# Two products instead of three for mixture-of-experts tiles of at most 64 rows, chosen by branches on TensorE, VectorE and ScalarE

## The chip, the cores and the metric

One core of one Trainium2 chip runs the whole program. The metric is the device time of one execution in microseconds, median of three runs. The traces come from one further, profiled execution.

## The reference, cut to what matters

An attention block with a memory term gives 2304 rows of 512 numbers. Two mixture-of-experts layers follow; each sends every row to one of 8 experts and scales the expert's result by a gate:

```python
expert_idx = np.argmax(logits, axis=1)
gate_w = probs[np.arange(N), expert_idx]
for e in range(E):
    mask = expert_idx == e
    h = np.maximum(x[mask] @ w1[e], 0.0)      # 512 -> 1024
    out[mask] = gate_w[mask, None] * (h @ w2[e])   # 1024 -> 512
```

On the inputs used, the reference sends these numbers of rows to the experts: layer 1: 14, 70, 440, 370, 0, 749, 11, 650; layer 2: 104, 380, 548, 438, 276, 112, 310, 136.

## The kernel before, in words

The attention part comes first. Then each layer (L = 0 and 1) runs in steps of one tile: 128 rows of one expert, gathered by index. The experts' rows are padded to whole tiles, so each layer has 22 tiles on these inputs. The largest expert comes first, the second largest last, the others in order of their index. The program is written for up to 28 steps a layer; from step 18 on each step stands in a branch on the real number of tiles (lines 1646 and 1726).

Products are made in three parts to keep float32's accuracy: each operand is split into a high part and a low rest, and the product is high x Wh, high x Wl, low x Wh. `mms` (line 1253) issues them: 4 blocks of the inner dimension times 3 for each half of the hidden layer (24 matmuls of 128x128 by 128x512 into `ph0` and `ph1`), and 8 blocks times 3 (24 matmuls into `py`). The plane of the weights (two are kept) is chosen at run time by a register, `pv`, so each matmul has a register operation ahead of it (lines 1219 and 1253).

A step of `step()` in order, on TensorE: 12 matmuls into `ph0`; 6 into `ph1`; four transposes of the first hidden half (`hT(0)`, line 1365); in layer 1 four transposes of the last result for the second layer's routing (`yT_pe`, line 1306); 6 more into `ph1`; four transposes of the next tile's rows (`xT_pe`, line 1192); 3 matmuls into `py`; `hT(1)`; 21 matmuls into `py`. ScalarE applies ReLU from PSUM (lines 1395 and 1416) and writes high parts (line 1196), VectorE writes low parts (line 1197), both also split the next expert's weights (lines 903 and 906). `end()` scales `py` into `ysb` on ScalarE (line 1355) and GpSimd sends it out: to a scratch tensor in layer 1, by an indirect DMA to the result in layer 2.

The order of the work on each engine is the order of the program text (a manual schedule); the framework places the semaphores. The weights' splits and loads stand in branches on flags held in registers (lines 1264, 1280, 1284). The registers are loaded from bit words in `fw` (line 1202) at steps 4 and 16. In the trace `PEldq`, `ACTq` and `DVEq` are the sequencers, the parts of the engines that run register operations, branches and semaphore instructions; their time isn't counted as busy.

Of the kernel before, what the change touches and what calls it, by code (L numbers as in the profile page):

```python
# [389 lines left out]
def tile_kernel(ctx, tc, q, k, v, M_prev, z_prev, beta, emb, tau, w1a, w2a, wg, w1b, w2b, out):  # L390
# [4 lines left out]
    P = 128  # L395
# [43 lines left out]
    fw = ctile([P, 2, 3], "fw", I32)  # L439
# [287 lines left out]
    def finish1(L, NI, psc, psi, new, st):  # L727
# [3 lines left out]
        ci = rtile([P, E], "ci", I32)  # L731
# [17 lines left out]
        V.tensor_copy(nt, ci)  # L749
        yield  # L750
# [75 lines left out]
    def finish2(L, st):  # L826
# [7 lines left out]
        V = nc.vector  # L834
        stt, ts = V.scalar_tensor_tensor, V.tensor_scalar
# [8 lines left out]
        V.tensor_tensor(out=c8, in0=c8, in1=ea.unsqueeze(1).to_broadcast([P, E, E]), op=ALU.mult)  # L844
        V.tensor_tensor(out=w["mo"], in0=s0, in1=nt, op=ALU.add)
        V.tensor_reduce(out=w["code"], in_=c8, axis=AX.X, op=ALU.add)
# [333 lines left out]
    class Bufs:  # L1180


        def __init__(self, where):
            self.x = (where(0), where(1))
            self.h = ((where(2), where(3)), (where(4), where(5)))
            self.hs = (where(6), where(7))
# [7 lines left out]
    def hilo(ps, hl):  # L1194
        hi, lo = hl
        nc.scalar.activation(out=hi, in_=ps, func=AF.Copy)  # L1196
        nc.vector.tensor_tensor(out=lo, in0=ps, in1=hi.bitcast(F32), op=ALU.subtract)  # L1197

    NK = (KD, KF)

# [5 lines left out]
    class Step:  # L1206


        def __init__(self, L, t):
            self.L, self.t = L, t  # L1210
            if 0 < t <= NE:
                self.pv = steps[L, 0].pv
            elif t:
                g, k = divmod(t - TW, BW)
                if k == 0:
                    self.words = words(fw[0:1, g, 0:3], [ACT_, DVE_, POOL_]) + words(fw[0:1, g, 2:3], [PE_])
                else:
                    self.words = steps[L, t - 1].words
                self.pv = nc.snap((self.words[3] >> k) & 1, engines=[PE_], min_val=0, max_val=1)
            else:  # L1220
                self.pv = 0 if L == 0 else nc.values_load(ini[0:1, 1, 4:5], engines=[PE_], min_val=0, max_val=1)
            self.spl = [[], []]

# [20 lines left out]
        def mms(self, i, ps, lhs, n0, qs, first=False, last=False):  # L1244
            L, t = self.L, self.t
            ps_ = slice(self.pv, self.pv + 1) if isinstance(self.pv, int) else bass.ds(self.pv, 1)
            for q_ in qs:
                kk, m = divmod(q_, 3)
                hi, lo, col = lhs(kk)
                w = 1024 * kk + n0 if i == 0 else 512 * kk  # L1250
                W = (Wh, Wl, Wh)[m][i][:, ps_, w:w + 512].rearrange("p o n -> p (o n)")
                x = (hi, hi, lo)[m]
                mm = nc.tensor.matmul(ps, x[:, col:col + P], W, start=(first and q_ == qs[0]), stop=(last and q_ == qs[-1]))  # L1253
# [6 lines left out]
            self.lm = (i, mm.ins)  # L1260

        def splits(self, i, cs, parts="hl"):

            with tc.If(self.fv[i] > 0):  # L1264
                for c in cs:
                    for x in parts:
# [5 lines left out]
                        if last_mm.get(i) is not None:  # L1272
                            tc.add_manual_dep(ins, last_mm[i].name, SYNC, reason="buffer free")
# [89 lines left out]
    def hT(i, b):  # L1363
        for kk in range(4):
            nc.tensor.transpose(pts[i][:, P * kk:P * kk + P], b.hs[i][:, P * kk:P * kk + P], ident)  # L1365
        hilo(pts[i], b.h[i])
# [5 lines left out]
    def next_step(L, t):  # L1372
        n = steps[L, t] = Step(L, t)
# [3 lines left out]
    def step(L, t):  # L1377
# [7 lines left out]
        lx = lambda kk: (*x, P * kk)  # L1385
        lh = lambda kk: (*b.h[kk // 4], P * (kk % 4))
        begin(L, t)
        s.gemm(0, ph0, lx, 0, 0, 3)
        yield
        s.gemm(0, ph0, lx, 0, 3, 9)  # L1390
        yield
        s.gemm(0, ph0, lx, 0, 9, 12)
        if split2:
            s.splits(0, (0, 1))
        nc.scalar.activation(out=b.hs[0], in_=ph0, func=AF.Relu)
# [8 lines left out]
        s.gemm(0, ph1, lx, 512, 0, 6)  # L1404
        hT(0, b)
# [8 lines left out]
        s.gemm(0, ph1, lx, 512, 6, 12)  # L1414
        last_mm[0] = s.lm[1]
        nc.scalar.activation(out=b.hs[1], in_=ph1, func=AF.Relu)
# [6 lines left out]
        if more:  # L1423
            hilo(psx, b.x)
        if rt2:
            route2_iov()
        s.gemm(1, py, lh, 0, 0, 3)
        if split2:
            s.splits(0, (2,), "h")
        hT(1, b)  # L1430
        if split2:
            s.splits(0, (2,), "l")
        if more:
            next_step(L, t + 1)
        yield
        s.gemm(1, py, lh, 0, 3, 6)
# [8 lines left out]
        s.gemm(1, py, lh, 0, 6, 9)  # L1445
# [23 lines left out]
        for q_ in range(9, 24, 3):  # L1469
            yield  # L1470
            s.gemm(1, py, lh, 0, q_, q_ + 3)
        last_mm[1] = s.lm[1]
# [24 lines left out]
    def flags_words(st):  # L1497
        yield
        x = rtile([P, 2, 3], "fx3", BF16)
        nc.vector.tensor_tensor(out=x, in0=st["fl"][:, 4:7].unsqueeze(1).to_broadcast([P, 2, 3]), in1=pw.unsqueeze(2).to_broadcast([P, 2, 3]), op=ALU.mult)  # L1500
        yield
        nc.tensor.matmul(pm1[:, 400:406], ones, x.rearrange("p g i -> p (g i)"), start=True, stop=True)
        nc.vector.tensor_copy(fw.rearrange("p g i -> p (g i)"), pm1[:, 400:406])
# [56 lines left out]
    b = Bufs(lambda i: Wh[0][:, 1, 512 * i:512 * i + 512] if i < 6 else None)  # L1560
    s = steps[0, 0] = Step(0, 0)
    lx = lambda kk: (*b.x, P * kk)
    lh = lambda kk: (*b.h[kk // 4], P * (kk % 4))
# [29 lines left out]
    x0 = tuple(fp.tile([P, 512], F32R, name=f"x0{i}") for i in range(2))  # L1593
# [3 lines left out]
    bufs = Bufs(lambda i: fp.tile([P, 512], F32R, name=f"b{i}") if i < 6 else hs_[i - 6])  # L1597
# [4 lines left out]
    nc.scalar.activation(out=b.hs[0], in_=ph0, func=AF.Relu)  # L1602
    nc.scalar.activation(out=b.hs[1], in_=ph1, func=AF.Relu)
# [25 lines left out]
    last_mm[0] = last_mm[1] = s.lm[1]  # L1629
# [21 lines left out]
    lx = lambda kk: (*x0, P * kk)  # L1651
    lh = lambda kk: (*b.h[kk // 4], P * (kk % 4))
# [45 lines left out]
    nc.scalar.activation(out=b.hs[0], in_=ph0, func=AF.Relu)  # L1698
# [59 lines left out]
```

## Time and profile before

| | |
|---|---|
| median of 3 runs | 886.68 us (885.24 to 887.39) |
| the profiled execution's own time | 885.27 us |
| its span, first to last instruction | 883.5 us |
| TensorE busy | 854.2 us, 97% of the span |
| TensorE's mean granted clock | 0.993 |
| VectorE, ScalarE, GpSimd busy | 508.7, 473.8, 276.9 us |

The profiled execution's time is 1.8 us above its span and 1.4 us below the median. TensorE's busy share is taken over pipelined matmuls whose ends are modelled, so what a step costs is better read from the distance between the starts of two steps.

### The profile page before, as it was taken

The page shows a single profiled execution, that of the slowest core. Times are in us where ns is not written, and L with a number is a line of the kernel's source. Part 1 is how long each engine was busy: PE and PEld are TensorE (multiplying, and loading weights), DVE is VectorE, ACT ScalarE, POOL GpSimd, SP SyncE. Part 2 cuts the span into 40 slices and gives each one's busy share as a digit, 9 for nine tenths or more (in the row PEclk, how much of TensorE's full clock was granted, in tenths as well). Part 3 has the DMA queues.
Part 4 walks back from the last instruction along what each step waited for, and adds up shares of the span by engine and source line. Part 5 has one row for each costly group of instructions (what it writes and reads, how often), then busy time and mean ns, then how long its engine had stood idle before and what let it go on. Part 6 is the DMA issues. An engine that isn't in the chain of part 4 may idle for free. (4 is left out here: it accounts for less than half of the span.)

```text
span 883.5 us, 20598 instructions
## 1 busy us (share of the span) xinstructions
PE 854.2 (97%) x5187; PEld 671.8 (76%) x5187; DVE 508.7 (58%) x1593; ACT 473.8 (54%) x940; POOL 276.9 (31%) x375
## 2 busy tenths in 40 slices
PE   5999999999999999999999999989989999999996
PEld 2777777777777787877888777867868888888885
DVE  5766577577686865487446666534466314463520
ACT  3666756767658454485454634522466425564531
POOL 5457747446432112312121221211132212321221
PEclk9999999999999999999999999999999999999998
DMA  8424454424225265286324125112587314483111
GB/s 132 83 45 96 84 161 111 72 42 104 40 96 193 67 228 185 72 290 219 141 97 162 57 81 197 46 45 72 205 274 279 125 46 160 136 305 124 45 38 40
DMA packets 139812, 110.29 MB, mean 125 GB/s; under 512 B 107258, under 2 KB 107258, under 8 KB 139652
## 3 DMA queue, kind: packets, MB, share of 16 engines
q1 hardware_dynamic: 129252, 85.03, 33.3%
q0 software_dynamic: 8032, 23.22, 8.0%
q8 instruction: 52, 0.85, 0.4%
q14 instruction: 108, 0.88, 0.3%
q10 hardware_dynamic: 2368, 0.30, 0.2%
HBM read 90.32 MB, written 19.25 MB: 124 GB/s over the span
## 5 line engine op out<-in xcount | busy, mean ns | idle before, releaser
L1253 PE MATMUL py<-Wh,b 128*128 (+1 forms) x688 | 240.7, 406 | 2.6 <-DVE b L1197 2.2
L1253 PE MATMUL ph<-Wh,b 128*128 (+1 forms) x672 | 227.8, 400 | 0.4 <-ACTq L1264 0.3
L906 DVE TENSOR_TENSOR Wl<-stg,Wh 128x1024 f32 (+1 forms) x120 | 145.4, 1224 | 81.8 <-ACT Wh L903 70.6
L1253 PEld LDWEIGHTS py<-Wh,b 128*128 128x128 f32 x688 | 129.3, 188 | 32.6 <-issue 5.0
L1253 PEld LDWEIGHTS ph<-Wh,b 128*128 128x128 f32 x672 | 126.8, 189 | 26.8 <-ACTq L1264 0.8
L903 ACT ACTIVATE Wh<-stg 128x1024 f32 (+1 forms) x120 | 125.6, 1057 | 25.8 <-DVEq L1264 6.7
L1253 PE MATMUL py<-Wl,b 128*128 (+1 forms) x344 | 134.8, 392 | 0.0
L1253 PE MATMUL ph<-Wl,b 128*128 (+1 forms) x336 | 131.8, 392 | 2.0 <-DVEq L1264 1.8
L1197 DVE TENSOR_TENSOR b<-pt,b 128x512 fp32r<-128x512 f32 x86 | 59.4, 690 | 105.4 <-ACT b L1196 102.3
L267 ACT ACTIVATE att<-psat 128x512 f32<-128x512 f32 (+1 forms) x144 | 66.5, 462 | 76.0 <-PE psat L265 75.5
L288 PE MATMUL psav<-vb,att 128*128 128x128 f32 (+1 forms) x640 | 93.5, 281 | 0.8 <-ACT att L267 0.7
L288 PEld LDWEIGHTS psav<-vb,att 128*128 128x128 f32 x640 | 80.1, 191 | 17.8 <-ACT att L267 6.4
L1360 POOL DMA_INDIRECT out_dram<-ysb,xca x21 | 26.8, 1278 | 192.4 <-ACTq L1264 122.9
L1196 ACT ACTIVATE b<-pt 128x512 fp32r<-128x512 f32 x86 | 51.4, 598 | 61.7 <-PE pt L1365 56.7
L1253 PEld LDWEIGHTS ph<-Wl,b 128*128 128x128 f32 x336 | 63.7, 190 | 14.6 <-DVEq L1264 2.5
L248 ACT ACTIVATE a<-a,mx 128x128 f32<-128x128 f32 (+3 forms) x128 | 71.0, 555 | 5.6 <-DVE mx L213 5.4
L1253 PEld LDWEIGHTS py<-Wl,b 128*128 128x128 f32 x344 | 64.9, 189 | 9.9
L1355 ACT ACTIVATE ysb<-py,xca 128x512 f32<-128x512 f32 x42 | 28.8, 686 | 76.6 <-PE py L1253 65.7
L213 DVE CUSTOM_DVE_ANT_0 a<-pss,wmask 128x128 f32<-128x128 f32 (+3 forms) x128 | 60.8, 481 | 14.2 <-PE pss L235 13.2
L1162 POOL DMA_INDIRECT xg<-x_scratch,idx x48 | 54.9, 1144 | 38.4 <-POOL xca L1349 10.7
L1477 POOL DMA_DIRECT2D x_scratch<-xcb x21 | 11.9, 565 | 163.1 <-DVEq L1264 62.0
L265 PE MATMUL psat<-ident,a 128*128 128x128 f32 x320 | 56.2, 276 | 0.7 <-ACT a L248 0.5
(377 smaller groups left out, 1243.0 us busy)
## 6 DMA issues: line engine op xcount, KB each, us to landing
stg<-in_moe_w_dram SPq DMA_DIRECT2D x120, 512.0 KB
x_scratch<-ysb POOLq DMA_DIRECT2D x22, 256.0 KB
qkn<-in_q_dram SPq DMA_DIRECT2D x64, 72.0 KB
qkn<-in_k_dram SPq DMA_DIRECT2D x60, 72.0 KB
vb<-in_v_dram SPq DMA_DIRECT2D x32, 128.0 KB
x_scratch<-xb SPq DMA_DIRECT2D x16, 256.0 KB
x_scratch<-stg SPq DMA_DIRECT2D x11, 258.0 KB
xg<-x_scratch,idx POOLq DMA_INDIRECT x48
```

Source lines behind the costliest of these rows:

```text
L213: nc.vector.tensor_tensor_reduce(out=out, in0=ps, in1=mask, scale=-0.125, scalar=bound, op0=ALU.add, op1=ALU.min, accum_out=m)
L248: nc.scalar.activation(out=a[:, 0:N], in_=a[:, 0:N], func=AF.Exp, scale=-1.0, bias=mx, accum_out=rs_t[pi][:, c, j:j + 1])
L265: nc.tensor.transpose(ps[:, 128 * i:128 * i + 128], x, ident)
L267: nc.scalar.activation(out=att[:, 0:N], in_=ps[:, 0:N], func=AF.Copy)
L288: nc.tensor.matmul(av_t[pi][:, c, j:], att[:, 128 * kb:128 * kb + 128], vn[:, kb, j:, 0:D], start=(kb == 0), stop=(kb == c))
L903: return nc.scalar.activation(out=chunk(Wh, c, wv), in_=stg[:, c].unsqueeze(1), func=AF.Copy).ins
L906: return nc.vector.tensor_tensor(out=chunk(Wl, c, wv), in0=stg[:, c].unsqueeze(1), in1=chunk(Wh, c, wv).bitcast(F32), op=ALU.subtract).ins
L1162: return nc.gpsimd.indirect_dma_start(out=rows_of(t), out_offset=None, in_=rows, in_offset=bass.IndirectOffsetOnAxis(ap=idx[:, L, t:t + 1] ...
L1196: nc.scalar.activation(out=hi, in_=ps, func=AF.Copy)
L1197: nc.vector.tensor_tensor(out=lo, in0=ps, in1=hi.bitcast(F32), op=ALU.subtract)
L1253: mm = nc.tensor.matmul(ps, x[:, col:col + P], W, start=(first and q_ == qs[0]), stop=(last and q_ == qs[-1]))
L1355: nc.scalar.activation(out=ysb, in_=py, func=AF.Copy, scale=xc[:, 0:1])
```

## The change

Where a tile has at most 64 rows, the low part is written into columns 64 to 127 of the stationary block that holds the high part in columns 0 to 63. One matmul with Wh then gives high x Wh in rows 0 to 63 and low x Wh in rows 64 to 127; one more with Wl adds high x Wl to rows 0 to 63. That is 32 matmuls a tile instead of 48. The hidden halves are added by a matmul with `fold` (two unit matrices stacked) where other tiles transpose; the result's halves are added on VectorE in `end()`. High and low parts now share a tile `[P, 4, 2 * P]`; ReLU moves from the copies after `ph0` and `ph1` to the copies after `hT`.

Which form a tile takes is a new bit in a fourth flag word, made in `finish2`. It is read into registers on TensorE (`hp`), VectorE (`hv[0]`) and ScalarE (`hv[1]`). Both forms stand in the program behind branches (`either`). Steps 0 to 3 of each layer and step 17 of the first have no branch. With the counts above the short tiles are steps 6, 11, 15 and 21 of the first layer and 4, 11, 15, 17 and 21 of the second: 9 of the 35 steps that carry the branches.

```diff
+    def hilo(ps, hl, relu=False, hv=None):
+        nc.scalar.activation(out=hl[:, :, 0:P], in_=ps, func=AF.Relu if relu else AF.Copy)
...
+            with tc.If(hv[0] < 1) as cmp:
+                lo(P, P)
+            with cmp.Else():
+                lo(HT, HT)
...
+    HQ = ((0, 1, 3, 2, 5, 4, 7, 6), (0, 2, 4, 6, 1, 3, 5, 7, 9, 11, 13, 15, 8, 10, 12, 14))
...
+        def pe_flags(self):
+            if self.t <= NE:
+                return
+            g, k = divmod(self.t - TW, BW)
+            if k == 0:
+                self.pwords = words(fw[0:1, g, 2:4], [PE_])
+            else:
+                self.pwords = steps[self.L, self.t - 1].pwords
+            bit = lambda i: nc.snap((self.pwords[i] >> k) & 1, engines=[PE_], min_val=0, max_val=1)
+            self.pv = bit(0)
+            if self.hv is not None:
+                self.hp = bit(1)
...
+        def either(self, whole, part):
+            if self.hv is None:
+                whole()
+                return
+            with tc.If(self.hp < 1) as cmp:
+                whole()
+            lm = self.lm
+            with cmp.Else():
+                part()
+            self.lm = lm + self.lm
...
-        nc.scalar.activation(out=ysb, in_=py, func=AF.Copy, scale=xc[:, 0:1])
+            with tc.If(hv[1] < 1) as cmp:
+                whole()
+            with cmp.Else():
+                nc.scalar.activation(out=ysb[0:HT], in_=py[HT:P], func=AF.Copy)
+            with tc.If(hv[0] > 0):
+                nc.vector.tensor_tensor(out=ysb[0:HT], in0=py[0:HT], in1=ysb[0:HT], op=ALU.add)
+                nc.vector.tensor_scalar(out=ysb[0:HT], in0=ysb[0:HT], scalar1=xc[0:HT, 0:1], scalar2=None, op0=ALU.mult)
...
+    def hT2_pe(i, b):
+        for kk in range(4):
+            nc.tensor.matmul(pts[i][:, P * kk:P * kk + HT], b.hs[i][:, P * kk:P * kk + P], fold, start=True, stop=True)
...
+            s.either(lambda: s.gemm(0, ph0, lx, 0, 0, 12), lambda: s.gemm2(0, ph0, lx, 0, HQ[0], True))
...
+        s.either(lambda: (s.gemm(0, ph1, lx, 512, 0, 6), hT_pe(0, b)), lambda: (s.gemm2(0, ph1, lx, 512, HQ[0][0:4]), hT2_pe(0, b)))
+        hT_ev(0, b, s.hv)
...
+        s.either(lambda: s.gemm(0, ph1, lx, 512, 6, 12), lambda: s.gemm2(0, ph1, lx, 512, HQ[0][4:], True))
...
+            next_step(L, t + 1)
+            hilo(psx, b.x, False, steps[L, t + 1].hv)
...
+        s.either(lambda: (s.gemm(1, py, lh, 0, 0, 3), hT_pe(1, b)), lambda: (s.gemm2(1, py, lh, 0, HQ[1][0:4]), hT2_pe(1, b)))
+        hT_ev(1, b, s.hv)
...
+            next_flags(L, t + 1)
...
+        if rt2 or s.hv is None:
+            s.either(lambda: s.gemm(1, py, lh, 0, 3, 6), lambda: s.gemm2(1, py, lh, 0, HQ[1][4:6]))
...
+            a, n = (6, 6) if rt2 else (3, 4)
+            s.either(lambda: s.gemm(1, py, lh, 0, a, 24), lambda: s.gemm2(1, py, lh, 0, HQ[1][n:], True))
```

## Rows read from the trace of the kernel before

**Rows 1.** The page's first part: busy us, share of the span, instructions.

```profile
PE 854.2 (97%) x5187; PEld 671.8 (76%) x5187; DVE 508.7 (58%) x1593; ACT 473.8 (54%) x940; POOL 276.9 (31%) x375
```

**Rows 2.** Windows, one step of each layer: PE, PEld, DVE, ACT, POOL, clock, DMA, GB/s.

```profile
425.19:438.82 13.63, 13.63 (x77) 11.15 (x76) 7.60 (x27) 4.33 (x8) 2.49 (x5) 1.00 0.45 157
703.78:716.08 12.30, 12.30 (x61) 10.18 (x60) 2.08 (x3) 3.57 (x6) 2.21 (x3) 1.00 0.14 43
```

**Rows 3.** Timeline of the step from 703.78: start us, us, engine, line, what.

```profile
709.96 0.60 ACT L1416 ACTIVATE hs<-ph 128x512 f32<-128x512 f32 x1 [0.85 <-PE ph L1253]
...
710.84 0.60 PE L1365 MATMUL pt<-ident,hs 128*128 128x128 f32 x4
...
711.19 0.48 PE L1253 MATMUL py<-Wh,b 128*128 x1
...
711.48 0.60 ACT L1196 ACTIVATE b<-pt 128x512 fp32r<-128x512 f32 x1 [0.43 <-PE pt L1365]
```

**Rows 4.** Register operations of that step's second half: ns min/median/max, first to last start.

```profile
L1219 PEldq ALU_OP  x2: 36/36/36, 710.6 to 710.7; - x2
L1219 PEldq FUSED_REGOPS  x1: 68/68/68, 710.8 to 710.8; - x1
...
L1253 PEldq FUSED_REGOPS  x3: 55/60/60, 711.0 to 711.3; - x3
```

**Rows 5.** Line 1253 from 704.22 to 707.45 us: matmuls and register operations.

```profile
L1253 PE MATMUL ph<-Wh,b x10: 389/389/389, 704.2 to 707.2; 128*128 x10
...
L1253 PEldq FUSED_REGOPS  x2: 55/55/55, 704.2 to 707.4; - x2
```

**Rows 6.** Timeline of ScalarE, 703.7 to 707.5 us.

```profile
704.12 0.69 ACT L1355 ACTIVATE ysb<-py,xca 128x512 f32<-128x512 f32 x1 [4.34 <-PE py L1253]
706.76 0.60 ACT L1395 ACTIVATE hs<-ph 128x512 f32<-128x512 f32 x1 [1.95 <-PE ph L1253]
```

**Rows 7.** Line 1264, a skipped branch on ScalarE, 704 to 705 us.

```profile
L1264 ACTq COMPARE_BRANCH  x1: 45/45/45, 704.1 to 704.1; - x1
L1264 ACTq EVENT_SEMAPHORE  x1: 17/17/17, 704.8 to 704.8; - x1
```

**Rows 8.** Line 1646 on TensorE's sequencer, whole trace.

```profile
L1646 PEldq COMPARE_BRANCH  x6: 68/75/3469, 535.7 to 593.7; - x6
...
L1646 PEldq EVENT_SEMAPHORE  x1: 51/51/51, 593.5 to 593.5; - x1
```

**Rows 9.** Timeline, TensorE's way out of the branch at line 1646.

```profile
591.72 0.17 PE L1339 MATMUL pm<-acc,ones 128*128 128x8 bf16 x1
...
594.60 0.50 PE L1253 MATMUL ph<-Wh,x 128*128 x1 [2.72 <-ACTq L1646]
```

**Rows 10.** Timeline of a layer 1 step (521.2 to 536.4 us), second hidden half.

```profile
528.93 0.60 ACT L1416 ACTIVATE hs<-ph 128x512 f32<-128x512 f32 x1 [1.22 <-PE ph L1253]
...
530.76 0.48 PE L1253 MATMUL py<-Wh,b 128*128 x1
```

**Rows 11.** Timeline of TensorE where flag words are loaded, layer 2, step 3.

```profile
645.97 0.49 PE L1253 MATMUL py<-Wh,b 128*128 x1 [0.32 <-issue]
```

**Rows 12.** Line 1202, the loading of flag words on ScalarE, whole trace.

```profile
L1202 ACTq TENSOR_LOAD <-fw x4: 703/705/711, 334.9 to 797.7; - x4
```

**Rows 13.** Timeline, a layer 1 step in which VectorE splits weights.

```profile
385.91 0.60 PE L1306 MATMUL pm<-ident,ysb 128*128 128x128 f32 x4
...
386.04 3.68 DVE L906 TENSOR_TENSOR Wl<-stg,Wh 128x1024 f32 x3
...
390.37 0.50 PE L1253 MATMUL py<-Wh,b 128*128 x1 [0.90 <-DVE b L1197]
```

**Rows 14.** Windows, columns as in rows 2: after a long wait, and around a shorter one.

```profile
653.50:656.90 3.40, 3.40 (x10) 2.63 (x9) 2.45 (x2) 1.73 (x2) 2.52 (x3) 0.50 1.00 339
403.00:407.00 4.00, 2.69 (x22) 1.73 (x21) 3.53 (x9) 2.32 (x4) 1.46 (x4) 1.00 0.85 286
```

**Rows 15.** DMA queues: packets, MB, share of 16 engines.

```profile
q8 instruction: 52, 0.85, 0.4%
```

More of the change, by code (lines that the diff above doesn't have):

```diff
@@ L749, in finish1 @@
         V.tensor_copy(nt, ci)
+        V.tensor_scalar(out=ci, in0=psc, scalar1=63.0, scalar2=None, op0=ALU.add)
         yield
@@ L1242, in gemm, with gemm2, mms @@
             self.mms(i, ps, lhs, n0, range(a, b), a == 0, b == 3 * NK[i])
-        def mms(self, i, ps, lhs, n0, qs, first=False, last=False):
+        def either(self, whole, part):
[8 more added lines that the diff above has]
+            self.lm = lm + self.lm
+        def gemm2(self, i, ps, lhs, n0, qs, last=False):
+            for q_ in qs:
+                self.mms(i, ps, lhs, n0, (q_,), q_ == 0, last and q_ == qs[-1], 2)
+        def mms(self, i, ps, lhs, n0, qs, first=False, last=False, per=3):
             L, t = self.L, self.t
@@ L1372, in next_step, with next_flags @@
     def next_step(L, t):
-        n = steps[L, t] = Step(L, t)
+        steps[L, t] = Step(L, t)
+    def next_flags(L, t):
+        n = steps[L, t]
+        n.pe_flags()
         if t > 2:
@@ L1413, in step @@
             rank_ev(t - 2)
[L1414 to L1416 removed]
+        s.either(lambda: s.gemm(0, ph1, lx, 512, 6, 12), lambda: s.gemm2(0, ph1, lx, 512, HQ[0][4:], True))
+        last_mm[0] = s.lm
+        nc.scalar.activation(out=b.hs[1], in_=ph1, func=AF.Copy)
         yield
@@ L1592, in tile_kernel @@
     fp = ctx.enter_context(tc.tile_pool(name="fp", bufs=1, side="right", reuse_waits="tile"))
-    x0 = tuple(fp.tile([P, 512], F32R, name=f"x0{i}") for i in range(2))
+    x0 = fp.tile([P, 4, 2 * P], F32R, name="x0")
     hs_ = [fp.tile([P, 512], F32, name=f"hs{i}") for i in range(2)]
@@ L1596, in tile_kernel @@
     ysb = fp.tile([P, DM], F32, name="ysb")
-    bufs = Bufs(lambda i: fp.tile([P, 512], F32R, name=f"b{i}") if i < 6 else hs_[i - 6])
+    fold = fp.tile([P, HT], F32, name="fold")
+    nc.gpsimd.tensor_tensor(out=fold, in0=ident[:, 0:HT], in1=ident[:, HT:P], op=ALU.add)
+    bufs = Bufs(lambda i: fp.tile([P, 4, 2 * P], F32R, name=f"b{i}") if i < 3 else hs_[i - 3])
     b.hs = bufs.hs
@@ L1601, in tile_kernel @@
     C = chain0()
-    nc.scalar.activation(out=b.hs[0], in_=ph0, func=AF.Relu)
-    nc.scalar.activation(out=b.hs[1], in_=ph1, func=AF.Relu)
+    nc.scalar.activation(out=b.hs[0], in_=ph0, func=AF.Copy)
+    nc.scalar.activation(out=b.hs[1], in_=ph1, func=AF.Copy)
     lo(4)
@@ L1697, in tile_kernel @@
     run(C, n1[1])
-    nc.scalar.activation(out=b.hs[0], in_=ph0, func=AF.Relu)
+    nc.scalar.activation(out=b.hs[0], in_=ph0, func=AF.Copy)
     s.gemm(0, ph1, lx, 512, 0, 6)
@@ L1702, in tile_kernel @@
     s.gemm(0, ph1, lx, 512, 6, 12)
-    nc.scalar.activation(out=b.hs[1], in_=ph1, func=AF.Relu)
+    nc.scalar.activation(out=b.hs[1], in_=ph1, func=AF.Copy)
     run(C, n1[3])
```

126 lines of the change are left out of this document (76 added, 50 removed).

## The prediction

> **What bounds the kernel now.** I read the page's busy times first: TensorE is busy for 97% of the span [rows 1]. Then windows cut at the first matmul of each step: a step lasts 13.63 us in layer 1 and 12.30 us in layer 2, and TensorE is busy through all of both [rows 2]; VectorE and ScalarE have room there. So the order on TensorE sets the end, and what counts is what its sequencer hands it without a gap. A step of layer 2 is 48 matmuls and 12 transposes; four transposes take 711.19 - 710.84 = 0.35 us [rows 3], so a matmul costs (12.30 - 3 x 0.35) / 48 = 0.234 us. Third I read the sequencer. Its register operations show how far ahead it runs: none starts between 704.2 and 707.4 us while ten matmuls with Wh run on [rows 5]; it goes on when ScalarE's first hidden half is done at 706.76 + 0.60 = 707.36 [rows 6]. So it runs far ahead of the array until an instruction waits, and then starts anew with almost no lead. At the second hidden half the lead is the smallest: ScalarE is done at 709.96 + 0.60 = 710.56, the two ALU operations and one fused operation of `pv` follow from 710.6, the next matmul's from 711.0 [rows 4], and that matmul starts at 711.19, as soon as the transposes let it [rows 3]. There is hardly a tenth to spare at this place in layer 2.
>
> **What is removed.** A short tile loses 16 matmuls: 16 x 0.234 = 3.75 us. Nine of the 44 tiles are short, 33.7 us in all, the ceiling. A `fold` matmul in place of a transpose I cost at nothing, between -0.05 and +0.1 us a tile, as it streams half the columns.
>
> **What a branch on TensorE costs when it is passed.** A compare on its sequencer takes 68 ns where it falls through [rows 8]. Each `either` is a compare and, for a whole tile, a jump over the other form: about 0.13 and 0.2 us with the gap behind them, an estimate from the 68 to 75 ns of rows 8 and from the 0.1 us between the starts in rows 4. Where the sequencer has its lead this is hidden under matmuls at 0.234 us each. A step has five `either` in layer 2, six in layer 1.
>
> **What a branch costs at its end.** Consumers on other engines wait for counts, so both arms must end on the same count; the shorter arm is padded. The trace shows such a pad on a skipped branch: the compare runs at 704.1, the pad only at 704.8 [rows 7], when the copy ahead of it (704.12 + 0.69 = 704.81) has ended [rows 6]. The pad waits for all earlier work of its own engine. TensorE has one too [rows 8], so far only at a way out. On ScalarE and VectorE, which work one instruction after the other, this is nearly free. On TensorE it takes the lead away: the array runs empty before the sequencer goes on.
>
> Count the instructions of the arms. First `ph0` product: 12 whole, 8 short. First `ph1` part with `hT`: 10 and 8. Second: 6 and 4. First `py` part with `hT(1)`: 3 + 4 = 7 whole, 4 + 4 = 8 short. Layer 1's middle part: 3 and 2. Rest: 18 and 10, or 21 and 12. So short tiles are padded at every branch but one, and every whole tile is padded at that one, right behind `hT(1)`, where the lead is smallest.
>
> **A whole tile.** The pad passes when the transposes' semaphore does, about 711.44 (ScalarE takes their result at 711.48 [rows 3]). Then come the pad, 0.05 [rows 8] with 0.06 behind it; the jump over the other arm, 0.2; two register bits in place of one, each about 0.33 (710.6 to 711.0 with the gap, less what the next operation overlaps) [rows 4]; the next compare, 0.13; the matmul's own register operation and weights, 0.25. Sum 1.35: the matmul that started at 711.19 starts at about 712.79, 1.6 us late. Nothing later in the step can win that back, as TensorE has no other gap. In layer 1 the same chain hangs on the same transposes. 26 whole tiles behind branches x 1.6 = 41.6 us. Without the pad the chain starts at 710.6 and gives 711.85, 0.65 late in layer 2; in layer 1 ScalarE is done at 529.53 and the matmul starts at 530.76 [rows 10], so 1.24 us are there and nothing is lost. [...]
>
> **A short tile.** A pad without flags behind it costs what is left of the last matmul, 0.389 - 0.234 [rows 5], the pad 0.11, the compare 0.2 and 0.15 to 0.25 for the next matmul: about 0.6 us. Four of them in layer 2, five in layer 1; and only four matmuls (0.94 us) lie between the last `fold` and the first use of the second half's high part, which takes ScalarE 0.60 and two semaphores: 0.3 us late. Left of 3.75: 1.05 in layer 2, 0.45 in layer 1. Sum 5 x 1.05 + 4 x 0.45 = 7.1 us gained, against 9 x 3.4 = 30.6 with no pads. I take 7.1, as rows 7 show the waiting pad.
>
> **What is moved.** The flag words of steps 4 and 16 are now loaded ahead of the copies of the next tile's rows, on ScalarE and VectorE too. A load takes 0.70 us on ScalarE [rows 12], there are now two, and register work with them: about 1.8 us ahead of `hT(1)`'s copy, which has 1.1 us of slack. 0.7 us four times, 3 us with TensorE's second load; today one load of it shows as 0.32 us [rows 11]. Bounds 0 and 8.
>
> **The add of halves on VectorE.** `ysb` now also has VectorE as a writer, so its readers wait for VectorE's branch or pad, in program order behind the weights' splits. In a step with splits VectorE is at them from 386.04 to 389.72, while TensorE transposes `ysb` at 385.91 [rows 13]: it would wait 3.8 us, and win back the 0.9 us that it loses today at 390.37. Of these 2.9 us I take 2.5, as longer steps give VectorE time to catch up, twice in layer 1 (405 us looks alike [rows 14]); 5 us, bounds 0 and 15. Layer 2 has only the DMA out behind it. VectorE's branches around the low parts and the few operations in `finish2` lie beside TensorE's work; I cost them at nothing, 3 us if that cover fails.
>
> **The sum.** 41.6 + 3 + 5 - 7.1 = +42.5 us. Against the profiled execution's 885.3 us (span 883.5 and 1.8 around it) that is 928 us; the median of the runs is 1.4 us above that execution, which is inside the error.
>
> **A rule on jumps.** The longest way of line 1646 costs 3469 ns on the sequencer [rows 8] and TensorE stands still for 2.72 us [rows 9]. That jump passes six steps. The 52 instruction packets [rows 15], taken as TensorE's, hold 0.85 MB; with its 10,374 matmuls and weight loads [rows 1] and some 1,900 register operations that is about 236 instructions a packet, and the longest arm (21 matmuls, some 65 instructions) is well below one packet. So I cost a jump at 0.2 us. [...]
>
> **The rivals.**
> - No drain: the pads are folded into the arms' last instructions. For it: a matmul that ends a group carries a count already. Against it: rows 7. Then 13 x 0.65 + 3 + 5 - 30.6 = -14 us: 871 us, faster. It decides from the point where the wait after `hT(1)` is below 0.7 us a whole tile.
> - The whole tiles' pad is absent and the short ones' stay: 8.5 + 3 + 5 - 7.1 = +9: 895 us.
> [...]
> - Jumps that cross a packet's border stall like the far one. A whole tile jumps over some 120 of 236 instructions, so one jump in every second step: 17 x 2.7 = 46 us on 871: 917 us.
>
> **How the numbers follow.** My forecast 0.60, with its own range 908 to 945; no drain 0.22; short pads alone 0.10; the clock 0.05; the jumps 0.03. The range 868 to 945 leaves out the clock, half of what lies around 871 on its lower side and a little above 945, about 0.18. A measurement here tells a change from none at about 0.3%, 2.7 us. Faster by more: 0.22, all from the no-drain case. Within: 0.05, its upper edge and the lower edge of 895. Slower: 0.73.
>
> **What would show it.** Right: on TensorE's sequencer one event-semaphore instruction per whole step behind `hT(1)`, and a gap of about 1.6 us between these transposes and the next matmul; whole steps of layer 2 of 13.9 us instead of 12.30; short ones near 11.2; the clock at 1.00 there. Wrong: whole steps of 12.3 to 13 us, or short steps below 9.5, which would mean arms without a drain; half clock in many steps; compares of 3 us on TensorE.

## The result and the profile after

The changed kernel takes 892.22 us (median of 5 runs, 890.91 to 892.89) against 886.97 us before (885.24 to 887.39): ratio 1.0059, 95% interval 1.0044 to 1.0074, so 5.3 us slower. The direction was forecast, the size was not: 928 us was +41. (The direction came out for other reasons than the forecast's, see below.) The profiled execution has a span of 890.7 us, 7.2 more than before.

From the page of the changed kernel, busy times and one DMA queue (packets, MB, share of 16 engines):

```profile
PE 842.0 (95%) x5123; PEld 650.5 (73%) x5123; DVE 514.1 (58%) x1621; ACT 474.9 (53%) x940; POOL 269.8 (30%) x376
...
q8 instruction: 72, 1.18, 0.6%
```

TensorE is busy 12.2 us less [rows 1] and yet ends 7.2 us later: waits have come in between its products. Windows of the changed kernel (columns as in [rows 2]): two whole steps of layer 2, a short one, a short step of layer 1, and step 7 of layer 1:

```profile
734.97:747.69 12.72, 12.57 (x62) 10.24 (x60) 8.11 (x9) 7.39 (x10) 2.81 (x3) 1.00 0.44 123
747.69:760.46 12.77, 12.74 (x62) 10.29 (x61) 4.57 (x6) 7.55 (x10) 2.22 (x3) 1.00 0.52 158
725.25:734.97 9.72, 9.72 (x54) 7.29 (x53) 1.54 (x3) 3.57 (x6) 2.22 (x3) 1.00 0.19 57
355.86:366.76 10.90, 10.90 (x70) 8.17 (x68) 2.60 (x12) 4.35 (x8) 2.49 (x5) 1.00 0.17 52
378.67:397.23 18.56, 14.55 (x78) 11.05 (x76) 16.06 (x31) 14.26 (x19) 2.50 (x5) 1.00 0.84 272
```

A whole step of layer 2 takes 0.45 us more than in [rows 2], a short one 2.6 less; step 7 of layer 1 took 14.78 before. Cutting every step at its first `ph0` product in both traces and subtracting gives the whole account. Short steps lie at 5, 6, 11, 15 of layer 1 and 9, 12, 16, 18 of layer 2: eight, not nine, since the ninth short tile falls on step 3 of layer 2, where no branch stands. Nor are these the steps that the section on the change lists. They fit another order of experts than the one told there: in layer 1 the expert with 650 rows is first and that with 749 last, in layer 2 those with 438 and 380. So 8 of the 35 steps with branches are short and 27 whole, and in layer 1 two short steps come one behind the other, just ahead of step 7.

| part of the span | us against before |
|---|---|
| up to the first step | +0.6 |
| layer 1: four short steps | -8.5 |
| layer 1: steps 7, 8, 16 | +8.9 |
| layer 1: all others | +3.5 |
| layer 2: four short steps | -10.0 |
| layer 2: all others | +10.7 |
| from the last step's start on | +2.1 |

(The last line differs between executions. From the last step's start to the end took 19.6 us in the three profiled kernels without a short step in layer 2, and 19.6 to 22.0 in those with them. So it isn't shown whether the change has a part in these 2.1 us.)

**No drain.** The first thing to look for was an event semaphore behind `hT(1)`, the sign of a drain: a wait of TensorE's sequencer until all earlier work of its own engine has ended. TensorE's timeline in a whole step of layer 2, and the register operations of the same place (count, ns min/median/max, first to last start), both of the changed kernel:

```profile
742.03 0.60 PE L1441 MATMUL pt<-ident,hs 128*128 128x128 f32 x4
742.78 0.49 PE L1318 MATMUL py<-Wh,b 128*128 x1
```

```profile
L1261 PEldq ALU_OP  x3: 32/36/36, 742.0 to 742.3; - x3
L1261 PEldq FUSED_REGOPS  x1: 58/58/58, 742.2 to 742.2; - x1
L1261 PEldq MOVE  x1: 37/37/37, 742.4 to 742.4; - x1
```

The next product starts 0.75 us behind the first transpose, against 0.35 in [rows 3], and in between stand the register operations of two bits, not a semaphore. The branches themselves, over the whole trace:

```profile
L1291 PEldq COMPARE_BRANCH  x340: 65/169/368, 338.5 to 879.9; - x170
```

There is no EVENT_SEMAPHORE on that line, and the longest branch takes 0.37 us, where the far one of [rows 8] took 3.47.

TensorE's sequencer does carry 53 event semaphores on lines of products that the kernel before doesn't have: 45 on line 1318 and 8 on line 1446, ahead of `fold`. Two of them lie in the step above (line 1318, 740.5 to 745 us):

```profile
L1318 PEldq EVENT_SEMAPHORE  x2: 51/51/51, 741.1 to 744.4; - x2
```

They are no drains: where the trace names a releaser for these 53 it is VectorE or ScalarE, never TensorE, and in 46 of them a product is still running when the semaphore is passed. One of the two stands ahead of the first `py` product, one ahead of the first that reads the second hidden half, neither between `hT(1)` and the next product. High and low parts now share a tile; in the kernel of experiment 5, where products of high parts don't wait for low ones, the 45 are 17.

**Two new costs.** The first is in the short step that starts at 725.25 above. TensorE's timeline:

```profile
728.00 1.10 PE L1446 MATMUL pt<-fold,hs 128*128 128x64 f32 x8
728.91 0.42 PE L1318 MATMUL ph<-Wl,b 128*64 x1
...
731.35 1.00 PE L1446 MATMUL pt<-fold,hs 128*128 128x64 f32 x8
732.16 0.66 PE L1318 MATMUL py<-Wl,b 128*64 x2
```

Four `fold` products leave eight records and take 0.91 and 0.81 us from start to next start; four transposes take 0.35. The second is step 7 of layer 1, behind the short steps 5 and 6. Timeline of all engines, part:

```profile
377.14 4.19 ACT L909 ACTIVATE Wh<-stg 128x1024 f32 x4 [0.62 <-DVE b L1208]
...
378.67 0.39 PE L1318 MATMUL ph<-Wh,b 128*128 x1
...
379.19 5.00 DVE L912 TENSOR_TENSOR Wl<-stg,Wh 128x1024 f32 x4
380.48 0.50 PE L1318 MATMUL ph<-Wl,b 128*128 x1 [1.42 <-DVE Wl L912]
...
381.51 0.60 ACT L1428 ACTIVATE ysb<-py 64x512 f32<-64x512 f32 x1
...
385.25 0.68 DVE L1430 TENSOR_TENSOR ysb<-py,ysb 64x512 f32<-64x512 f32 x1
...
386.04 0.48 DVE L1431 TENSOR_SCALAR ysb<-ysb,xca 64x512 f32<-64x512 f32 x1
...
386.57 0.66 PE L1371 MATMUL pm<-ident,ysb 128*128 128x128 f32 x4 [1.09 <-DVE ysb L1431]
```

These rows show two waits. Step 7 begins at 378.67, and its second product needs weights whose low part VectorE has not yet split: 1.42 us. And the previous tile's `ysb`, whose products ended near 379, is added on VectorE only at 385.25, behind four splits and the routing, so the transposes of `ysb` stand 1.09 us more.

### The profile page after: what moved, and what is told of

Read it like the earlier page. It is cut to its first block, busy times and chain, and to the rows that moved or that the text cites. A ratio compares the mean times of both kernels' runs of the same rounds, so it can differ in the third digit from the quotient of the medians.

```text
span 890.7 us, 21738 instructions
## 1 busy us (share of the span) xinstructions
PE 842.0 (95%) x5123; PEld 650.5 (73%) x5123; DVE 514.1 (58%) x1621; ACT 474.9 (53%) x940; POOL 269.8 (30%) x376
## 5 line engine op out<-in xcount | busy, mean ns | idle before, releaser
L1318 PE MATMUL py<-Wh,b 128*128 (+1 forms) x624 | 214.3, 406 | 9.0 <-DVE b L1208 3.8
L1318 PE MATMUL ph<-Wh,b 128*128 (+1 forms) x608 | 208.8, 399 | 0.4 <-ACTq L1329 0.2
L1318 PEld LDWEIGHTS py<-Wh,b 128*128 128x128 f32 x624 | 116.7, 188 | 40.5 <-issue 13.6
L1318 PE MATMUL ph<-Wl,b 128*128 (+2 forms) x336 | 130.5, 396 | 5.0 <-DVE Wl L912 3.0
L1318 PEld LDWEIGHTS ph<-Wh,b 128*128 128x128 f32 x608 | 114.9, 189 | 26.9 <-issue 1.1
L1318 PE MATMUL py<-Wl,b 128*128 (+2 forms) x344 | 126.9, 393 | 0.2 <-ACT b L1203 0.2
L1208 DVE SCALAR_TENSOR_TENSOR b<-pt,b 128x512 fp32r<-128x512 f32 (+1 forms) x86 | 55.1, 641 | 108.3 <-ACT b L1203 96.0
L1318 PEld LDWEIGHTS ph<-Wl,b 128*128 128x128 f32 (+1 forms) x336 | 60.1, 179 | 19.7 <-DVE Wl L912 4.1
L1318 PEld LDWEIGHTS py<-Wl,b 128*128 128x128 f32 (+1 forms) x344 | 60.4, 178 | 12.7 <-ACT b L1203 1.6
L1420 ACT ACTIVATE ysb<-py,xca 128x512 f32<-128x512 f32 x34 | 23.3, 686 | 62.5 <-PE py L1318 49.0
```

Of the source, the lines that this page charges most:

```text
L1208: nc.vector.scalar_tensor_tensor(out=o, in0=x, scalar=0.0, in1=h, op0=ALU.max, op1=ALU.subtract)
L1318: mm = nc.tensor.matmul(o, x, W, start=(first and q_ == qs[0]), stop=(last and q_ == qs[-1]))
```

## The experiments

All were timed beside the kernel before; what a kernel differs from the changed one is the difference of their ratios to it (1.0059 with its interval for the changed one), times 887 us.

**1. All arms whole.** The short bit is always 0.

```
- scalar1=6, scalar2=1, op0=ALU.arith_shift_right, op1=ALU.bitwise_and
+ scalar1=6, scalar2=0, op0=ALU.arith_shift_right, op1=ALU.bitwise_and
```

> The bit that names a short tile is zero for every tile, so every branch takes its whole arm, with 48 matmuls a tile; nothing else is changed. Theory A, from the trace of the changed kernel: no arm ends in a drain, and an undisturbed whole step costs about 0.45 us more in layer 2 (18 x 0.45 = 8.1) and 0.2 us more in layer 1 (17 x 0.2 = 3.4), the flag words, their loads and VectorE's late low parts some 6 us together: 903 to 906 us, no transpose of ysb waits over 0.5 us. Theory P, the prediction's: each of 35 whole tiles pays 1.6 us at a drain behind hT(1): 35 x 1.6 + 8 on 887 is 951 us. Theory F, the branches are free and only what follows short tiles costs: 887 to 889 us.

Measured: 904.51 us, ratio 1.0212 (1.0197 to 1.0227), +18.5 us. Theory A holds; the prediction's 951 is far off. One part of it misses: transposes of `ysb` do wait over 0.5 us, without one short tile. Who TensorE's transposes wait for here (us in total, times, longest):

```profile
PE pm L1371 <- DVEq L1429: 2.7, 3, 1.8
```

Line 1429 is VectorE's condition in `end`; that it is passed is enough. Steps 8 and 14 of layer 1 take 17.07 and 14.54 us here, 17.10 and 14.60 in the changed kernel: what they lose isn't made by short tiles.

**2 and 3. One layer only.** `self.hv` is set for `L == 1`, or for `L == 0`, alone.

> Layer 1 is put back to whole tiles without branches; layer 2 keeps all of the change. Theory A: layer 1's steps sum to 3.9 us more than before in the changed kernel (short steps 8.5 us shorter, the others 12.4 longer, above all steps 7, 8 and 16, which wait for VectorE), so without its branches 892.2 - 3.9 + 0.5 for the wider flag words = 889 us, and the steps of layer 1 are as in the kernel before within 0.6 us. Theory P (1.6 us a whole tile): layer 2 alone costs 14 x 1.6 - 4 x 1.05 + 1.5 = 20: 907 us. If the two layers shared the loss evenly, 889.6; if short tiles gain in layer 1, above 893.

> Layer 2 is put back to whole tiles without branches; layer 1 keeps all of the change. Theory A: layer 2's branch steps and their flags cost 11.1 us in the changed kernel and its four short steps give 10.0 back, so without them 892.2 - 1.1 = 891 us, and steps 7, 8 and 16 of layer 1 are as long as in the changed kernel (18.6, 17.1, 17.6 us). Theory P (1.6 us a whole tile): 13 x 1.6 - 4 x 0.45 + 6.5 = 25: 912 us.

Measured: 1.0024 (1.0012 to 1.0035), +2.1 us, and 1.005 (1.0037 to 1.0063), +4.4 us; their sum is 6.5 against 5.2 for both, within the intervals. Layer 1 is back to its old sum in the first (313.2 us, 313.0 before), and steps 7, 8 and 16 take 18.56, 17.12 and 17.57 us in the second. Each layer makes its own loss.

**4. Bits early.**

```
         s.either(... the first ph0 product ...)
+        if more:
+            s.ahead_flags()      # TensorE's bits (and words) of step t + 1
...
-            self.pv = bit(0)     # behind hT(1)
+            self.pv, self.hp = o.npv, o.nhp
```

> TensorE takes the two register bits of the next step, and the flag word of steps 4 and 16, right behind the first ph0 product, where its sequencer has matmuls queued, instead of behind hT(1). Theory A: behind hT(1) only the compare and one fused operation are left, which the four transposes hide; the 0.39 us between the last transpose and the next matmul go in 14 whole steps of layer 2 (5.5 us), 0.2 in its short ones, and most of the 1.0 us that TensorE waits there in steps 3 and 15: 884 to 886 us, faster than the kernel before by 1 to 3. Rival: the jump and the compare alone keep the next matmul late, so only half of it goes: 889 us. Rival: the sequencer has no lead at the new place either, and the gap moves with the bits: 892 us.

Measured: 888.05 us, ratio 1.0029 (1.0015 to 1.0042): 2.7 us faster than the changed kernel, below half of the 7 us that were expected. The first rival, at 889, is nearest by its time, not by its reason: the jump and the compare still stand there and the next product isn't late. Two whole steps of this kernel's layer 2:

```profile
699.66:711.95 12.29, 12.29 (x61) 10.19 (x60) 4.35 (x5) 3.90 (x7) 2.21 (x3) 1.00 0.55 175
746.35:758.89 12.54, 12.51 (x61) 10.25 (x60) 4.34 (x6) 7.33 (x10) 2.21 (x3) 1.00 0.53 163
```

The gap behind `hT(1)` has gone in both (the next product starts 0.36 us behind the first transpose). In the second a pause of 0.28 us ahead of the first `py` product is left, where the trace has VectorE's low part as the releaser, and in layer 2's steps 14 and 15 the full loss (13.80 and 13.92 us). So the place of the bits is one cause, not the only one. Step 3 of layer 1 went from 14.26 to 13.68: there it was TensorE's own load of the words. But step 4 behind it rose from 14.50 to 15.38, so layer 1 kept nothing of that.

**5. High parts first.** The products of the whole arm that read a high part are declared free of the low part's write.

```
+ if per == 3 and m < 2 and self.hv is not None:
+     tc.declare_no_dep(mm.ins, group=f"lo{'x' if i == 0 else kk // 4}_{L}_{t}", ...)
```

> The products of the whole arms that read only a high part no longer depend on VectorE's write of the low part, which now lies in the same tile; so the wait for VectorE moves from the first product of the second matrix to the third, where the kernel before had it. Nothing else is changed. Theory A: the first py product of a whole step behind a change of expert stands 0.9 to 1.1 us for VectorE's low part (at 680.6 and 790.7 us of the changed kernel's trace 1.09 and 0.93, in layer 1 at 390.9 and 407.8 1.34 and 0.97), and with two products more of cover about 0.45 us of each goes: 2 to 3 us, 889 to 890 us on a before of 887. Rival: the wait is for a VectorE that is simply late, with ScalarE's weights ahead of it, and comes back at the third product: 892 us.

Measured: ratio 1.0054 (1.0035 to 1.0073): no difference that can be told. The rival holds as far as the time goes; the waits of `py` for VectorE fell from 3.8 to 2.5 us in the trace.

**6. Halves left out.**

```
- nc.scalar.activation(out=ysb[0:HT], in_=py[HT:P], func=AF.Copy)
- with tc.If(hv[0] > 0): ...add and scale on VectorE...
+ nc.scalar.activation(out=ysb[0:HT], in_=py[0:HT], func=AF.Copy, scale=xc[0:HT, 0:1])
```

> The end of a step leaves the lower half of a short tile's products (the low parts' share) out of the result, so VectorE has no branch and no add there and ysb has ScalarE as its only writer. Theory A: in layer 1 the transposes of ysb wait for VectorE's branch or add behind the weights' splits (1.1 us in step 7, 1.8 in step 8, 0.7 in step 14, 1.7 in step 16 of the changed kernel); without it these 5.3 us go: 887 us on a before of 887; layer 2 stays as it is within 1 us. Rival: the transposes would wait for ScalarE's copy or the first py product for the low parts instead, so less than 2 us go: above 890.

Measured: 885.13 us, ratio 0.9998 (0.9987 to 1.001): 5.4 us less than the changed kernel, as expected (885.1 on a before of 884.6). Layer 1's steps sum to 312.0 us, 316.9 in the changed kernel: steps 7 and 16 fell by 1.2 and 1.9, step 14 is back at 13.63; step 8 stayed at 17.54, with a mean clock of 0.90 in it. Layer 2 didn't stay as it was: its steps 5 and 14, in which weights are split, fell from 13.92 and 13.70 to 13.02 and 12.76. So VectorE's condition costs 0.9 us in each of them as well, where the prediction had nothing.

**7. Steps 6 and 15 whole.**

```
- if (L, t) != (0, NT1 - 1):
+ if (L, t) not in ((0, NT1 - 1), (0, 6), (0, 15)):
```

> Steps 6 and 15 of layer 1, which are short in the changed kernel and are the ones in which the weights of the next expert are split, are whole without branches; all else keeps the change. Theory A: VectorE and ScalarE need some 15 us for a step with the splits of a whole expert, a short step gives them 11.9, so the rest is paid by the step behind it, with the first product with Wl 1.4 to 1.6 us late: with whole steps in their place step 7 falls from 18.56 to 15.7 and step 16 from 17.56 to 14.4, while steps 6 and 15 rise by 1.7 and 1.3: 892.2 - 2.9 - 3.2 + 3.0 = 889 us. Rival: step 7 is long by the weights' DMAs, which start earlier for the earlier steps; then it stays at 18.6 and the time rises to 895.

Measured: 886.2 us, ratio 1.0018 (1.0008 to 1.0028): 3.6 us faster with two short steps fewer. Its windows, steps 6, 7 and 16:

```profile
364.97:378.75 13.78, 13.78 (x77) 11.07 (x76) 11.61 (x27) 11.44 (x15) 4.26 (x5) 1.00 0.50 177
378.75:394.16 15.41, 13.84 (x77) 11.20 (x76) 13.53 (x27) 12.11 (x17) 2.50 (x5) 1.00 0.92 303
505.11:519.61 14.50, 14.01 (x80) 10.96 (x78) 9.73 (x30) 5.22 (x10) 2.50 (x6) 1.00 0.12 38
```

Beside them steps 7 and 16 of the kernel of experiment 6, short steps 6 and 15 but no halves on VectorE:

```profile
377.13:394.53 17.40, 14.21 (x77) 11.07 (x76) 15.47 (x30) 14.02 (x19) 2.49 (x5) 1.00 0.85 282
503.66:519.28 15.62, 14.01 (x80) 10.96 (x78) 10.66 (x34) 6.47 (x11) 2.50 (x6) 1.00 0.12 35
```

Step 7 needs 3.15 us less, step 16 3.06 less, at a price of 1.9 and 1.8 in steps 6 and 15. DMA is at 0.92 in step 7, busier than in the changed kernel (0.84), and yet the step is shorter: the rival falls.

But whole steps 6 and 15 take away the add of their halves too, so this experiment and the last overlap. By pairs: steps 6 and 7 last 28.41 us before, 29.06 with short steps and no halves, 30.47 in the changed kernel; steps 15 and 16 last 27.82, 27.96 and 29.92. So even without the halves the two short steps gain nothing: VectorE is late in the step behind (in step 7 of experiment 6's kernel TensorE waits 1.54 us for `Wl` and 1.65 ahead of the first `py` product). Most of what the pairs lose beyond that is the wait for the halves.

**8. Plain transposes for `fold`.** In `hT2_pe`, four `nc.tensor.transpose` with `ident`.

> In the short arms four plain transposes stand in place of the four products with the matrix fold, so the low parts' share of the hidden rows is left out. Theory A: a set of four fold products takes 0.91 and 0.81 us in a short step of layer 2 and four transposes take 0.35, so a short step gets 1.0 us shorter (8.7 in place of 9.72), eight of them 8 us, of which layer 1 keeps little in its steps 6 and 15 (VectorE): 885 to 887 us. Rival: the high part that ScalarE makes of the transposed rows is then what the next product waits for, and only half of it is saved: 888.

Measured: 884.44 us, ratio 0.9998 (0.9986 to 1.001), 5.4 us less. Its short step that answers to the one at 725.25:

```profile
720.57:729.41 8.84, 8.84 (x45) 6.45 (x44) 1.54 (x3) 3.57 (x6) 2.21 (x3) 1.00 0.19 62
```

0.9 us a step, a little under the 1.0 of TensorE's records. Of 8 x 0.9 = 7 us not all is kept: step 6 of layer 1 falls by 0.36 alone, and step 7 stays at 18.62.

**9. A drain where the prediction had one.**

```
             with tc.If(self.hp < 1) as cmp:
                 whole()
             lm = self.lm
-            with cmp.Else():
+            with (tc.If(self.hp > 0) if two else cmp.Else()):   # two: at py + hT(1) alone
                 part()
```

> At one of the five or six branches of a step, the one that holds the first py products and the transposes of hT(1), the two forms stand under two conditions, one after the other, in place of a condition and its else. The one that is passed then has an empty other side, and its pad waits on TensorE for TensorE's own count. So this kernel has the drain that the prediction put there. Theory A: a drain has the price that the prediction worked out, and what failed is only that a condition with an else needs none: a whole step of layer 2 lasts 13.9 us in place of 12.75, and the 27 whole tiles together with short ones cost 27 x 1.15 + 8 x 0.3 = 33 us more than the changed kernel: 1.043 of the kernel before, 920 to 928 us. Rival: the sequencer passes such a wait with little loss, the price itself was wrong: below 905 us.

Measured: 921.4 us, ratio 1.0398 (1.0384 to 1.0412): 30 us more than the changed kernel. A whole step of layer 2 and a short one, and the line of the second condition on TensorE's sequencer:

```profile
729.55:743.12 13.57, 12.53 (x61) 10.23 (x60) 1.81 (x3) 3.67 (x6) 2.21 (x3) 1.00 0.13 41
743.12:753.57 10.45, 9.82 (x53) 7.29 (x52) 1.54 (x3) 3.57 (x6) 2.21 (x3) 1.00 0.17 53
```

```profile
L1294 PEldq COMPARE_BRANCH  x3: 73/174/220, 736.6 to 749.4; - x3
L1294 PEldq EVENT_SEMAPHORE  x1: 51/51/51, 737.2 to 737.2; - x1
```

Now the semaphore is there. Over the whole trace it stands on the line of the second condition in each of the 27 whole steps, and on that of the first in each of the 8 short ones:

```profile
L1294 PEldq EVENT_SEMAPHORE  x27: 51/51/51, 349.7 to 905.7; - x27
L1291 PEldq EVENT_SEMAPHORE  x8: 51/51/51, 362.0 to 865.2; - x8
```

All 35 start 0.04 to 0.07 us behind the end of TensorE's last product: the array has run empty there.

Timeline of TensorE around it:

```profile
736.61 0.60 PE L1441 MATMUL pt<-ident,hs 128*128 128x128 f32 x4
738.25 0.47 PE L1318 MATMUL py<-Wh,b 128*128 x1 [1.04 <-ACT b L1203]
```

It passes when the transposes have ended, and only then do the bits, the compare and the next product follow: 1.64 us behind the first transpose, 1.29 more than in [rows 3], where the forecast had 1.6. (The row names ScalarE's copy of these transposes. In [rows 3] the same product starts before that copy does, so it doesn't need it.) The kernel also has 43 branch records more than the changed one; what they cost isn't separated from the wait. So the price was nearly right, the drain wasn't there.

**10. Halves on GpSimd.**

```
- nc.scalar.activation(out=ysb[0:HT], in_=py[HT:P], func=AF.Copy)
+ nc.scalar.activation(out=ysb[0:HT], in_=py[0:HT], func=AF.Copy)
+ nc.scalar.activation(out=bufs.hs[1][0:HT], in_=py[HT:P], func=AF.Copy)
- with tc.If(hv[0] > 0):   # nc.vector: add, scale
+ with tc.If(hv[2] > 0):   # nc.gpsimd: add, scale
```

> The halves of a short tile's result are copied by ScalarE and added and scaled on GpSimd, not on VectorE; the result is the full one. Theory A: GpSimd has no weights' splits in its queue, so the transposes of ysb in layer 1 wait no more, and all of the 5.4 us go that leaving the half out gave: ratio 0.999 to 1.002 to the kernel before, steps 8 and 14 of layer 1 at 17.5 and 13.7 us. Rival: GpSimd's add comes behind its gather (1.07 us) and is slow itself, and the transposes wait for it instead in short tiles: ratio 1.003 to 1.006.

Measured: ratio 1.018 (1.0156 to 1.0203), 902.73 us, worse than either theory. Who TensorE waits for in this kernel (us in total, times, longest; the execution profiled is the slowest of six, 908.14 us):

```profile
PE pm L1371 <- POOL ysb L1432: 11.9, 4, 5.4
```

and that line on GpSimd (ns min/median/max):

```profile
L1432 POOL TENSOR_SCALAR ysb<-ysb,xca x8: 1564/2426/3475, 371.4 to 864.0; 64x512 f32<-64x512 f32 x8
```

The scaling alone takes 2.4 us, against 0.48 on VectorE above. The transposes of `ysb` wait up to 5.4 us for it.

**11. Words early.** ScalarE, VectorE and GpSimd load the words of steps 4 and 16 behind `end` of steps 2 and 14.

> ScalarE, VectorE and GpSimd load the words of flags of steps 4 and 16 at the end of steps 2 and 14, not ahead of the copies of the next tile's rows in steps 3 and 15; TensorE loads its own where it did. Theory A: these loads hold up the copies in front of hT(1), so step 3 of layer 2 loses its 0.57 us and step 15 0.8 of its 1.2: 1 to 2 us in all, ratio 1.004. Rival: what TensorE waits for there is its own load of two words, which stays: no change, ratio 1.006.

Measured: ratio 1.0061 (1.0038 to 1.0085), no change; the rival holds. Step 3 of layer 2 stayed at 14.78 us, the changed kernel's value. With TensorE's words early as well (the next kernel) it took 13.84, with those alone 15.05, so both are needed there.

**12. All four together** (4, 5, 10, 11).

> All four changes at once: TensorE's bits behind the first ph0 product, the words loaded two steps ahead, the products of high parts free of the low parts' write, and the halves added on GpSimd. Theory A: the parts hang on different waits and add up: the ratio 1.0059 of the changed kernel less 0.0061 (sum), 0.003 (bits), 0.0015 (words) and 0.0005 (high parts) is 0.995, 4 us faster than the kernel before. Rival: what is taken from one wait comes back at the next (weights late after short steps): ratio 0.998 to 1.001.

Measured: ratio 1.0109 (1.0094 to 1.0124), a miss: GpSimd's add costs layer 1 as in 10 (its steps sum to 330.9 us, 313.0 before). But layer 2's steps sum to 260.6 us, 269.3 before, and its undisturbed whole steps are back at 12.3. (1.4 of these 8.7 us lie in step 4, where the kernel before shows a mean clock of 0.89 and this one 1.00.)

**13 and 14. Layer 2 alone, with the four edits, or with three and the halves on VectorE.**

> Layer 1 has whole tiles without branches, as before; layer 2 has the change with all four of the edits tried so far (bits early, words early, high parts free of the low parts' write, halves added on GpSimd). Theory A: with the four edits the steps of layer 2 sum to 8.7 us less than before (260.6 against 269.3 in the traces), and GpSimd's slow add (3.8 us in two operations) has only the DMA out behind it there; layer 1 and the start cost 0.5 us for the wider flag words: 8 us faster than the kernel before, ratio 0.990 to 0.992. Rival: the gain of layer 2 was made by the lull that layer 1's waits give the weights' DMAs, or is lost in a longer tail: ratio 0.995 to 0.999.

> The same kernel, but the halves are added on VectorE under its condition, as in the change. Theory A: in layer 2 nothing on TensorE reads the result rows, yet the pad of VectorE's passed condition stands between the splits and the low part that TensorE needs; in the steps with splits behind a short tile (27 and 36 counted from 0 over both layers, and those next to them) this costs 0.7 to 0.9 us each: 2 to 3 us more than with GpSimd, ratio 0.993 to 0.994. Rival: VectorE's branch in layer 2 lies beside TensorE's work as the prediction had it: no difference, ratio as the other kernel's within 0.001.

Measured: 879.1 us, 0.9937 (0.9918 to 0.9955), and 876.74 us, 0.9905 (0.9891 to 0.9919). Both are faster than the kernel before and the changed one; the second by 8 us against the kernel before. That VectorE's condition costs 2 to 3 us more, as theory A had it, doesn't show: its kernel has the lower median, but the intervals overlap and the two profiled executions came out the other way round (879.09 with VectorE, 876.65 with GpSimd). By steps both theories have a part: 5 and 14 are longer with VectorE (13.33 and 13.69 us against 12.77 and 12.66), steps behind short ones are shorter (step 13: 12.30 against 12.92). Three steps of the faster one, whole, short, whole, to set beside [rows 2] and the windows after:

```profile
691.87:704.22 12.35, 12.35 (x61) 10.25 (x60) 4.58 (x6) 3.62 (x7) 2.21 (x3) 1.00 0.51 173
716.50:726.20 9.70, 9.70 (x54) 7.29 (x53) 1.54 (x3) 3.57 (x6) 2.21 (x3) 1.00 0.17 57
738.49:750.77 12.28, 12.28 (x61) 10.18 (x60) 4.36 (x6) 7.63 (x10) 2.21 (x3) 1.00 0.49 166
```

Undisturbed whole steps cost what they did without branches, so the branches themselves can be hidden. With GpSimd the gain is 5.6 us, short of the 7 to 9 expected. Steps 5, 14 and 15 of layer 2, where weights are split, keep part of their loss in both (12.66 to 13.69 us against 12.27 to 12.68 before). With the halves on VectorE its condition has a share in 5 and 14 (experiment 6); the rest is open, and so is what each edit gives in layer 2 alone, which wasn't run. Of the 8.0 us by which layer 2's steps sum to less in the second kernel's trace (261.3 against 269.3) the four short steps give 10.0. Step 4 gives 1.4, but at a clock of 1.00 against 0.89, and step 0 takes 0.8 back at 0.82 against 0.90. The kernel before with its words and bits moved early wasn't run, so a part of the gain could be had without short tiles.

## Why the prediction was right or wrong

- **The step that failed** is "What a branch costs at its end", and with it the term 41.6. The prediction argued that both arms must end on the same count and that the shorter is padded by a wait. It took this from [rows 7], a condition on ScalarE whose other side is empty. In the changed kernel both sides hold products, no semaphore stands on the branch's line in 340 branch records, and the next product comes 0.40 us late, not 1.6. Experiment 9 makes one side empty and the semaphore appears in all 35 steps, with 30 us. The forecast of a whole step with a drain, 13.9 us, lies beside 13.57 measured. So the price was about right and the condition for it wrong. Whether the counts of unequal arms must be made even, and by what if not by a pad, no row shows; it stays open.
- **What came out by chance.** Slower was forecast because of drains; it came out because short steps give 18.5 us, not the ceiling of 33.7, and all other steps cost 23.1. The rival at 895 us, short pads alone, is nearest to 892 by its number, but short arms have no pads either: no semaphore on the branch's line in any of the eight.
- **The tiles** were counted as 26 whole and 9 short behind branches; they are 27 and 8. With the prediction's own terms that moves its sum by +2.7 us, so it isn't what failed.
- **The place was right.** `hT(1)` is where layer 2 has the least lead, and the register bits show there: 0.40 us (forecast 0.65 without pads), which goes when both bits are moved (experiment 4). In layer 1 undisturbed whole steps rose by 0 to 0.2, as forecast without pads.
- **Jumps** were right: the 340 branch records of the changed kernel take 0.065 to 0.37 us, with a median of 0.17, though the program grew from the 52 instruction packets of [rows 15] to 72. That a jump costs 0.2 us because the longest arm is well below a packet was the author's estimate: no run shows where a packet ends, nor what makes the far jump of [rows 8] take 3.47 us. None of the 340 comes near the 2.7 us of the rival in which jumps stall.
- **The clock**, with 0.05 of the chances, held in the two steps of experiment 9 shown above: 1.00 in both, with TensorE idle for 1.04 us ahead of the product at 738.25.
- **A short tile** was too low in the sum (0.45 to 1.05) and too high in the rival (3.4). Short steps are 2.6 to 2.8 us shorter where nothing else is late. The rival's size failed on `fold`, costed at -0.05 to +0.1 a tile and measured at +0.9.
- **What the halves cost on VectorE**, +5, was right: 5.4 in experiment 6. The mechanism too: `ysb` behind the splits, and the wait is paid for whole tiles as well (experiment 1). That the sizes agree so closely is in part luck: four waits in layer 1 in place of two, and 1.8 us in layer 2, where it had none.
- **The flag words**, +3, were about 1.2 in the steps 3 (0.6 in each layer), by another way than argued: in layer 1 TensorE's own load, not the copies on ScalarE and VectorE. What they cost in the steps 15 no run separates.
- **Missed altogether:** a short step leaves VectorE and ScalarE less time for the next expert's splits. Two of layer 1's short steps hold these splits and give back all that they gain, and with the wait for the halves more (experiment 7, 3.6 us). The prediction noted that both engines have room in a step of [rows 2], with 4.33 us of ScalarE, and didn't ask what a shorter step does where ScalarE has 14.26, as in step 7.
- **The rival without a drain** had the mechanism, and 871 us. From its -14 to the trace's +7.2 (+5.3 by the medians) lead short steps that give 18.5, not 30.6; steps 7, 8 and 16 of layer 1, which cost 8.9 where it had 5 for the halves; the other steps, 14.2 where it had 11.5 for bits and words; and 2.7 ahead of the first step and from the last one on.

## What to carry to other kernels

A wait that one row shows belongs to that row's circumstances: ask what in the code makes it (here an empty side of a condition) before it is multiplied by 26. Register work for a later branch belongs where the sequencer has products queued, not behind a dependency (experiment 4: the product behind `hT(1)` starts 0.36 us after the first transpose, not 0.75). And a step made shorter on the bounding engine must be checked against the steps in which its neighbours have the most work, not the mean step (steps 6 and 7 of layer 1: 30.47 us in the changed kernel, 28.41 before).

## What the runs showed of the hardware

- A float32 product of 128x128 by 64 columns leaves two records and takes about 0.2 us (0.91 and 0.81 for four); a float32 transpose of 128 columns takes 0.09 (0.35 for four). Half the columns weren't half the time.
- A multiplication of 64x512 float32 by a value per partition took 2.4 us on GpSimd (1.6 to 3.5, experiment 10) and 0.48 on VectorE (changed kernel).
- A stretch at the lower clock of [rows 14], 0.50, moves between executions of nearly the same program. Step 4 of layer 2 in the changed kernel, and step 16 of layer 1 in the kernel of experiment 5 (columns as before, the clock third from the end):

```profile
656.50:673.02 16.52, 14.71 (x61) 11.52 (x62) 10.46 (x11) 11.11 (x14) 4.03 (x3) 0.90 0.71 226
```

```profile
505.20:524.30 19.10, 15.74 (x79) 11.84 (x78) 11.78 (x35) 6.71 (x11) 2.50 (x5) 0.91 0.09 29
```

In the other kernel the same two steps took 14.87 and 17.56 us at a clock of 1.00. Both steps have a wait of TensorE of the same length in both kernels (1.73 us in the first, 1.75 in the second), and the clock fell around its end in one and not in the other. So one step of one execution can differ by 1.5 us for this alone, and a difference of that size in a step is to be read with the clock beside it.
